# A gated mix of sliding-window attention and a token-mixing MLP: x transposes by DMA into one tensor per block, weights on a second queue, and another order of the work

## The chip, the cores and the metric

The kernel runs on one core of a Trainium2 chip. The core has a matrix engine (TensorE, PE in the views), a vector engine (VectorE, DVE), a scalar engine (ScalarE, ACT), a general-purpose engine (GpSimd, POOL) and SyncE (SP), which here only issues DMAs; sixteen DMA engines move the data. Each engine runs its own instructions strictly in program order and waits at semaphores for the others. PE writes its results to PSUM, which has eight banks; everything else lies in SBUF.

The metric is the device time of one execution in microseconds.

## The reference, cut to what matters

x has 2048 rows (tokens) of 512 elements, bf16. Two results of x are mixed, row by row, with a gate.

```python
def _A_ref(x, wqkv, wo):            # 32 heads of 16, window of 256 keys
    qkv = (x @ wqkv).reshape(B, S, 3, H, Dh).transpose(2, 0, 3, 1, 4)
    q, k, v = qkv[0], qkv[1], qkv[2]
    scores = einsum("bhqd,bhkd->bhqk", q, k) * (Dh ** -0.5)
    mask = (i - j >= 0) & (i - j < 256)
    p = softmax(where(mask, scores, -1e9))
    o = einsum("bhqk,bhkd->bhqd", p, v)
    return o.transpose(0, 2, 1, 3).reshape(B, S, D) @ wo

def _B_ref(x, w1, b1, w2, b2):      # w1: 2048 x 1376, w2: 1376 x 2048
    h = layernorm(x)
    u = gelu(einsum("bsd,sf->bdf", h, w1) + b1)
    y = einsum("bdf,fs->bds", u, w2) + b2
    return y.transpose(0, 2, 1)

g = sigmoid((x * gate_w).sum(-1))
return g * _A_ref(x, ...) + (1 - g) * _B_ref(x, ...)
```

The MLP of B mixes tokens: its first product sums over all 2048 rows of h, so it can't start before the layer norm of every row is done.

## The kernel before, in words

**Tiles and stages.** Rows come in four blocks of 512 (index i) and sixteen groups of 128 (qb for queries, kb for keys). The stages are:

- *Loads.* x by rows into `xo` (`load_x`, line 330), wqkv in four pieces of 128 rows (`load_w`, line 337), w1 in twelve pieces (line 350), wo (line 355), all on SP's queue; a few small vectors on POOL's (line 359 and on). Later w2 (line 731) goes into the same buffer `wb` that held w1, piece by piece, once the chains that read w1 are done.
- *x transposed.* The projections need x with its columns on partitions, the tile `XT`, one tile of four column groups by 2048 rows. Block 0 is transposed by PE from `xo` (line 436) into PSUM and copied to `XT` by ACT or DVE (lines 419 and 420). Blocks 1 to 3 are transposed by DMA from DRAM (line 427), each into its 512 columns of every column group. `BYPE = 1` says how many blocks go by PE.
- *Projections* (`project`). For each block four chains for K, four for Q, four for V; a chain is a sum of four matmuls of 512 columns into one PSUM bank (`chain`, line 462). K is copied to `KT` and V to `VA` (lines 419, 420). Q is multiplied on DVE by two masks of alternating heads into `QZ` (line 502), so that one product with K gives two heads apart.
- *Attention.* For each group of queries qb and each half of the heads hf there are up to three key groups; each triple (qb, hf, kb) is called a piece, 90 in all. A piece is eight S matmuls (line 568) into two pairs of banks, two exps on ACT (line 587), a mask on the diagonal and on the far key group, by DVE (line 598) or POOL (line 602), and sixteen matmuls with V (line 623). The extra column of ones in `VA` gives the softmax's sums; a reciprocal (line 639) and a product (line 646) on DVE normalise into `on`, which has five buffers. A DMA transpose (line 657) puts it, transposed, over the rows of `xo` that are no longer needed.
- *Layer norm.* For each group of 128 rows `bn_stats` and `bn_aggr` on DVE (lines 517, 521), for each block an inverse root on POOL (line 527), then `h` on DVE or POOL (line 534).
- *MLP and end.* Eleven chains u of 16 matmuls (h by w1), each followed by a GELU of five steps on DVE and ACT (lines 312, 703, 708, 715, 720); sixteen chains y of 11 matmuls (w2 by the GELU's result); y is scaled and shifted (lines 310, 313), the chain a (o by wo) is added with the gate (line 754), and the result stored (line 759). The gate is 64 narrow matmuls on `XT` (line 668).

**What sets the order.** Each step is a `Task` with its engine or engines and an expected duration, its dependencies, a priority (lower goes first) and the buffers that it takes. `arrange` simulates the engines and at each step starts the task that can start earliest, within a patience the one of the lowest priority number; where a task may run on two engines it takes the one that finishes it first. The list that comes out is the program order on each engine. `LATENCY` is what it adds to a task's end before a dependent may start: 0.22 us for PE. `ORDER` holds the priorities and `BANKS` the PSUM banks that each kind of chain may take; S takes pairs from all eight. Waits between engines are put in afterwards, from the tiles that instructions read and write.

Of the kernel before, what the change touches and what calls it, by code (L numbers as in the profile page):

```python
# [8 lines left out]
BF16 = mybir.dt.bfloat16  # L9
# [99 lines left out]
def arrange(tasks, patience):  # L109
# [18 lines left out]
    while len(order) < len(tasks):  # L128
# [66 lines left out]
def kernel(  # L195
# [28 lines left out]
    BYPE = 1  # L224
# [8 lines left out]
    XT = sb.tile([P, 4, S], BF16, name="XT")  # L233
# [13 lines left out]
    QZ = sb.tile([P, NQ, 2, 4, SB], BF16, name="QZ")  # L247
# [51 lines left out]
    def add(*a, **k):  # L299
        t = Task(*a, **k)  # L300
        tasks.append(t)
        return t
# [16 lines left out]
    def load(name, emit, kb, q="SP", deps=(), prio=0.0, small=None, issue=0.5):  # L319
        landed[0] += kb / 370.0  # L320
        clock[0] += issue
# [11 lines left out]
    dwk = []  # L333

    def load_w(c):
        dwk.append(load(
            f"wqkv{c}", lambda: nc.sync.dma_start(wqkv[:, c, :], A_wqkv[c * P:(c + 1) * P, :]), 384, prio=0.001 * (c + 1)
        ))

    load_x(0)  # L340
    for c in range(4):
        load_w(c)
    for i in range(1, NSB):
        load_x(i)
# [79 lines left out]
    xt = {}  # L424
    for i in range(BYPE, NSB):
        def emit(i=i):
            nc.sync.dma_start_transpose(XT[:, :, i * SB:(i + 1) * SB], X[i * SB:(i + 1) * SB, :])
        xt[i, 0] = xt[i, 1] = add(f"xt{i}", {"SP": 7.5}, emit, [], 1.05 + 0.1 * i, lat=3.0)
    for i in range(BYPE):
        for c in range(2):  # L430
            b = bank("xt")

            def emit(i=i, c=c, b=b):
                g16 = buf(b).bitcast(BF16)
                return [
                    nc.tensor.transpose(
                        g16[:, (cc * 4 + t) * P:(cc * 4 + t + 1) * P],
                        xo[:, 4 * i + t, (2 * c + cc) * P:(2 * c + cc + 1) * P], ident[:],
                    )
                    for cc in range(2) for t in range(4)  # L440
                ]
# [372 lines left out]
```

## Time and profile before

| | us |
|---|---|
| median of 3 runs | 247.25 (247.23 to 247.72) |
| the profiled execution | 247.16 |
| its span | 245.0 |
| PE busy in it | 216.3 |
| ACT busy | 189.7 |
| DVE busy | 174.2 |
| POOL busy | 61.0 |

How to read the profile: the busy times are those of one profiled execution, on its one core. Its span runs from the first to the last instruction, and the execution's time is a little longer than that. The page cuts the span into 40 slices, 6.1 us each, and gives the busy share of an engine in each as a digit, 9 for 90% or more; PEclk gives PE's clock in the same way, as a share of full speed. In groups of instructions, "out<-in" names the tiles written and read, then come the count, the busy time, the mean duration of one in ns, and the idle time of that engine just before with what ended it. Matmuls overlap in PE's pipeline, so the mean duration of one is longer than its share of the busy time. A few matmul records are missing from the trace, which makes PE's busy time a little too small.

### The profile page before, as it was taken

The page shows a single profiled execution, that of the slowest core. Times are in us where ns is not written, and L with a number is a line of the kernel's source. Part 1 is how long each engine was busy: PE and PEld are TensorE (multiplying, and loading weights), DVE is VectorE, ACT ScalarE, POOL GpSimd, SP SyncE. Part 2 cuts the span into 40 slices and gives each one's busy share as a digit, 9 for nine tenths or more (in the row PEclk, how much of TensorE's full clock was granted, in tenths as well). Part 3 has the DMA queues.
Part 4 walks back from the last instruction along what each step waited for, and adds up shares of the span by engine and source line. Part 5 has one row for each costly group of instructions (what it writes and reads, how often), then busy time and mean ns, then how long its engine had stood idle before and what let it go on. Part 6 is the DMA issues. An engine that isn't in the chain of part 4 may idle for free. (4 is left out here: it accounts for less than half of the span.)

```text
span 245.0 us, 6531 instructions
## 1 busy us (share of the span) xinstructions
PE 216.3 (88%) x2809; PEld 105.1 (43%) x2856; DVE 174.2 (71%) x266; ACT 189.7 (77%) x214; POOL 61.0 (25%) x45
## 2 busy tenths in 40 slices
PE   7006998998999999999999999899999999999993
PEld 3002342634444444444444454345554444444541
DVE  3007899989996788889869688775765776667722
ACT  2004599797999998888999999888788888888821
POOL 8303597089165003333000000603003000030000
PEclk9655999979999999999999999999999999999998
DMA  6994999303011010541018116101003010101111
GB/s 185 225 276 100 287 351 345 100 3 46 1 24 24 0 24 3 165 201 24 0 24 293 54 24 237 24 0 46 24 21 67 24 46 23 47 21 46 45 36 50
DMA packets 26892, 21.66 MB, mean 88 GB/s; under 512 B 15760, under 2 KB 24464, under 8 KB 26864
## 3 DMA queue, kind: packets, MB, share of 16 engines
q1 hardware_dynamic: 26704, 21.24, 29.8%
q8 instruction: 22, 0.36, 0.6%
q0 software_dynamic: 160, 0.01, 0.5%
q14 instruction: 6, 0.05, 0.1%
HBM read 15.47 MB, written 2.10 MB: 72 GB/s over the span
## 5 line engine op out<-in xcount | busy, mean ns | idle before, releaser
L587 ACT ACTIVATE et<-ps 128x1024 bf16<-128x1024 f32 x180 | 170.7, 1039 | 19.1 <-PE ps L568 19.0
L598 DVE TENSOR_TENSOR et<-et,mask 128x2048 bf16<-128x2048 bf16 x47 | 59.0, 1255 | 14.0 <-ACT et L587 13.9
L602 POOL TENSOR_SCALAR_AFFINE_SELECT et<-et 128x2048 bf16<-128x2048 bf16 x13 | 26.1, 2008 | 125.1 <-PE pb L462 43.3
L623 PEld LDWEIGHTS <-et 128*128 128x128 bf16 x1440 | 46.9, 96 | 23.1 <-issue 5.0
L623 PE MATMUL pb<-VA,et 128*128 128x17 bf16 x1440 | 50.1, 171 | 0.8 <-DVE KT L420 0.6
L462 PE MATMUL pb<-XT,wqkv 128*128 128x512 bf16 x120 | 35.2, 402 | 17.0 <-DVE mv L521 15.0
L462 PE MATMUL pb<-h,wb 128*128 128x512 bf16 (+1 forms) x163 | 46.4, 381 | 1.3 <-issue 0.5
L462 PE MATMUL pb<-ug,wb 128*128 128x512 bf16 (+1 forms) x165 | 45.6, 380 | 1.3 <-DVE ot L754 0.4
L462 PEld LDWEIGHTS <-wb 128*128 128x128 bf16 (+2 forms) x352 | 27.8, 98 | 31.8 <-issue 8.7
L568 PE MATMUL ps<-QZ,KT 32*128 32x256 bf16 x720 | 36.1, 275 | 1.6 <-ACT et L587 1.2
L568 PEld LDWEIGHTS <-KT 32*128 32x128 bf16 x720 | 10.7, 92 | 33.4 <-ACT et L587 27.4
L462 PEld LDWEIGHTS <-wqkv 128*128 128x128 bf16 x128 | 11.1, 101 | 32.0 <-DVE mv L521 15.3
L534 POOL TENSOR_SCALAR h<-xo,mv,rstd 128x512 bf16<-128x512 bf16 x9 | 21.7, 2422 | 0.4
L754 DVE SCALAR_TENSOR_TENSOR ot<-pb,gg,bp 128x512 bf16<-128x512 f32 x16 | 12.0, 749 | 13.8 <-PE pb L462 11.7
L502 DVE TENSOR_TENSOR QZ<-pb,par 128x1024 bf16<-128x1024 f32 x16 | 19.2, 1219 | 3.6 <-PE pb L462 3.4
L462 PE MATMUL pb<-wo,xo 128*128 128x512 bf16 x57 | 17.4, 380 | 0.9 <-issue 0.3
L462 PE MATMUL pb<-wqkv,XT 128*128 128x512 bf16 x56 | 16.3, 398 | 0.8 <-issue 0.5
L313 DVE TENSOR_SCALAR bp<-pb,c,c 128x512 f32<-128x512 f32 x13 | 10.5, 808 | 6.1 <-PE pb L462 6.1
L419 ACT ACTIVATE XT<-pb 128x1024 bf16<-128x1024 bf16 x1 | 2.4, 2432 | 16.0 <-DMA XT<-in_A_x_dram 16.0
L646 DVE TENSOR_TENSOR on<-pb,rd 128x256 bf16<-128x256 f32 x32 | 13.6, 424 | 1.1
L517 DVE BATCH_NORM_STATS2 stats<-xo 128x6 f32<-128x512 bf16 x16 | 10.5, 671 | 2.4 <-DMA xo<-in_A_x_dram 2.4
L720 DVE SCALAR_TENSOR_TENSOR ug<-t,uf 128x512 bf16<-128x512 f32 (+1 forms) x11 | 7.5, 685 | 6.1 <-ACT t L715 6.1
(49 smaller groups left out, 106.7 us busy)
## 6 DMA issues: line engine op xcount, KB each, us to landing
wb<-in_B_w_dram SPq DMA_DIRECT2D x8, 512.0 KB, 8.3
wb<-in_B_w_dram SPq DMA_DIRECT2D x2, 2048.0 KB, 7.8
xo<-in_A_x_dram SPq DMA_DIRECT2D x4, 512.0 KB, 11.2
out_dram<-ot SPq DMA_DIRECT2D x16, 128.0 KB, 1.7
wqkv<-in_A_wqkv_dram SPq DMA_DIRECT2D x4, 384.0 KB, 6.4
wb<-in_B_w_dram SPq DMA_DIRECT2D x4, 352.0 KB, 9.3
wb<-in_B_w_dram SPq DMA_DIRECT2D x1, 1024.0 KB, 5.1
wo<-in_A_wo_dram SPq DMA_DIRECT2D x1, 512.0 KB, 4.6
```

The source lines that it names most:

```text
L313: return nc.vector.tensor_scalar(out=out_, in0=in_, scalar1=scale, scalar2=bias, op0=ALU.mult, op1=ALU.add)
L462: nc.tensor.matmul(buf(b)[:rows, :], lhsT=lhsT, rhs=rhs, start=(j == 0), stop=(j == n - 1))
L502: lambda k=k, b=b: nc.vector.tensor_tensor(out=QZ[:, i % NQ, :, k, :], in0=buf(b)[:, None, :].to_broadcast([P, 2, SB]), in1=par[:][:, :, N ...
L517: f"bs{t_}", {"DVE": 0.67}, lambda b=b, t_=t_: nc.vector.bn_stats(buf(b)[:], xo[:, t_, :]),
L534: return eng.tensor_scalar(out=h[:, t_, :], in0=xo[:, t_, :], scalar1=mv[:, t_, 0:1], scalar2=rstd[:, t_:t_ + 1], op0=ALU.subtract, op1=AL ...
L568: made.append(nc.tensor.matmul(buf(b2[r // 2])[:, (r % 2) * 512 + kk * 256:(r % 2) * 512 + kk * 256 + 256], lhsT=KT[32 * r:32 * r + 32, (k ...
L587: lambda j=j, b2=b2, e=e: nc.scalar.activation(out=buf(e)[:, j * 1024:(j + 1) * 1024], in_=buf(b2[j])[:], func=ACT.Exp, scale=SCALE),
L598: return nc.vector.tensor_tensor(out=view, in0=view, in1=mask[:, int(far), None, :].to_broadcast([P, 16, P]), op=ALU.mult)
L602: return nc.gpsimd.affine_select(out=buf(e), in_=buf(e), pattern=[[0, 16], [-1 if far else 1, P]], compare_op=ALU.is_gt if far else ALU.is ...
L623: made.append(nc.tensor.matmul(buf(o)[:, hl * DV:(hl + 1) * DV], lhsT=buf(e)[:, col:col + 128], rhs=VA[:, kb, head, :], start=(first and h ...
L646: lambda rd=rd, o=o, ob=ob, hf=hf: nc.vector.tensor_tensor(out=buf(ob)[:, hf * 256:(hf + 1) * 256].rearrange("p (h d) -> p h d", d=DH), in ...
L754: lambda bp=bp, b=b, ot=ot, qb=qb: nc.vector.scalar_tensor_tensor(out=buf(ot)[:], in0=buf(b)[:], scalar=gg[:, qb:qb + 1], in1=buf(bp)[:], ...
```

## The change

- *`arrange`.* Between two tasks of PE alone the 0.22 us are no longer added: a dependent PE task may follow at once.
- *`ORDER` and `BANKS`.* New priorities; more banks for most kinds of chain.
- *x transposed.* `XT` becomes four tiles, one for each block, and all four blocks are transposed by DMA. PE's transposes of block 0 and their copies go.
- *Loads.* wqkv comes in two pieces, the columns of Q and K together (1 MiB) and those of V (0.5 MiB), issued on ACT's queue. SP issues the transpose of block 0 first, then x 0, x 1, the transpose of block 1, x 2, x 3, four pieces of w1, the transposes of blocks 2 and 3, and the rest as before. The chains of K and Q depend on the first weight piece, those of V on the second.
- *Q layout.* In `QZ` the two masked copies of one Q chain lie side by side.
- *`h`.* Only DVE computes it.
- *The transpose of o* depends on all four h of its block in place of its own.
- One expected duration of y's evacuation on DVE is raised from 0.76 to 0.81.

```diff
@@ arrange
         for n, s in t.next:
             n.left -= 1
-            n.ready = max(n.ready, t.done if s is None else start + s)
+            if s is not None:
+                n.ready = max(n.ready, start + s)
+            elif list(n.engines) == ["PE"] == [e]:
+                n.ready = max(n.ready, end)
+            else:
+                n.ready = max(n.ready, t.done)
 ORDER = dict(
-    k=52.18, q=78.76, v=68.4, u=1.2, u_step=18.14, y=84.32, a=47.23, pv=6.7, s=5.8, to=100.63, gate=229.14,
-    lead=0.63, block=67.65, xt=-11.08, patience=0.17, m=60.31, ln=98.99, ev=60.19, gelu=2.68, w1=4.9,
+    k=-36.13, q=-39.5, v=-35.98, u=131.85, u_step=8.5, y=122.66, a=-17.68, pv=-21.07, s=-48.88, to=90.92,
+    gate=3.01, lead=-8.24, block=86.1, patience=0.13, m=46.84, ln=275.69, ev=8.39, gelu=97.56, w1=0.04,
 )
 BANKS = dict(
-    qkv=(5, 6, 7),
-    u=(6, 7),
-    y=(4, 5),
-    a=(4, 5),
-    pv=(6, 7),
-    to=(6, 7),
-    xt=(0, 1, 2, 3, 4, 5, 6, 7),
+    qkv=(4, 5, 6, 7),
+    u=(4, 5, 6, 7),
+    y=(7, 6, 5, 4, 3),
+    a=(2, 3, 4, 5, 6, 7),
+    pv=(0, 1, 2, 3, 4, 5, 6, 7),
+    xt=(4, 5),
 )
...
-    XT = sb.tile([P, 4, S], BF16, name="XT")
+    XT = [sb.tile([P, 4, SB], BF16, name=f"XT{i}") for i in range(NSB)]
...
-    QZ = sb.tile([P, NQ, 2, 4, SB], BF16, name="QZ")
+    QZ = sb.tile([P, NQ, 4, 2, SB], BF16, name="QZ")
...
-    dwk = []
-
-    def load_w(c):
-        dwk.append(load(
-            f"wqkv{c}", lambda: nc.sync.dma_start(wqkv[:, c, :], A_wqkv[c * P:(c + 1) * P, :]), 384, prio=0.001 * (c + 1)
+    def load_w(name, a, z, prio):
+        return load(
+            name, lambda: nc.scalar.dma_start(wqkv[:, :, a:z], A_wqkv[:, a:z].rearrange("(c p) n -> p c n", p=P)),
+            z - a, prio=prio, q="ACT",
+        )
+
+    xt = []
+
+    def load_t(i, prio):
+        landed[0] += 512 / 250.0
+        xt.append(add(
+            f"xt{i}", {"SP": 1.9}, lambda: nc.sync.dma_start_transpose(XT[i][:], X[i * SB:(i + 1) * SB, :]), [], prio,
+            lat=max(2.2, landed[0] - clock[0] - 1.9),
         ))
-
+        clock[0] += 1.9
+
+    load_t(0, 0.0)
+    dwk = load_w("wqk", 0, 2 * D, 0.0)
+    dwv = load_w("wv", 2 * D, 3 * D, 0.01)
     load_x(0)
-    for c in range(4):
-        load_w(c)
-    for i in range(1, NSB):
-        load_x(i)
+    load_x(1)
+    load_t(1, 0.015)
+    load_x(2)
+    load_x(3)
+    load_t(2, ORDER["w1"] + 0.045)
+    load_t(3, ORDER["w1"] + 0.095)
...
-    xt = {}
-    for i in range(BYPE, NSB):
-        def emit(i=i):
-            nc.sync.dma_start_transpose(XT[:, :, i * SB:(i + 1) * SB], X[i * SB:(i + 1) * SB, :])
-        xt[i, 0] = xt[i, 1] = add(f"xt{i}", {"SP": 7.5}, emit, [], 1.05 + 0.1 * i, lat=3.0)
-    for i in range(BYPE):
-        for c in range(2):
...
-            t = add(f"xt{i}{c}", {"PE": 0.55}, emit, [dx[i], k1], ORDER["xt"] + i, takes=[b])
-            xt[i, c] = copy_out(
...
@@ project
-                b, t = chain(f"v{t_}", mms, dwk + [xt[i, 0], xt[i, 1], warm, k5], prio, "qkv")
+                b, t = chain(f"v{t_}", mms, [dwv, xt[i], warm, k5], prio, "qkv")
...
-            b, t = chain(f"{kind}{k}_{i}", mms, dwk + [xt[i, 0], xt[i, 1], warm] + old, prio, "qkv")
+            b, t = chain(f"{kind}{k}_{i}", mms, [dwk, xt[i], warm] + old, prio, "qkv")
...
-                        out=QZ[:, i % NQ, :, k, :], in0=buf(b)[:, None, :].to_broadcast([P, 2, SB]),
+                        out=QZ[:, i % NQ, k, :, :], in0=buf(b)[:, None, :].to_broadcast([P, 2, SB]),
...
-                eng = nc.vector if engine[0] == "DVE" else nc.gpsimd
-                return eng.tensor_scalar(
+                return nc.vector.tensor_scalar(
...
-            hready.append(add(f"h{t_}", {"DVE": 0.41, "POOL": 0.75}, emit_h, [pw], ORDER["ln"] - 0.5 + i))
+            hready.append(add(f"h{t_}", {"DVE": 0.41}, emit_h, [pw], ORDER["ln"] - 0.5 + i))
...
-                            rhs=QZ[32 * r:32 * r + 32, (qb // 4) % NQ, :, k, (qb % 4) * P:(qb % 4 + 1) * P],
+                            rhs=QZ[32 * r:32 * r + 32, (qb // 4) % NQ, k, :, (qb % 4) * P:(qb % 4 + 1) * P],
...
-                rel[qb] + [hready[qb]], ORDER["to"], lat=2.5, uses=[ob],
+                rel[qb] + hready[4 * (qb // 4):4 * (qb // 4) + 4], ORDER["to"], lat=2.5, uses=[ob],
...
-            f"yb{qb}", {"ACT": 0.72, "DVE": 0.76},
+            f"yb{qb}", {"ACT": 0.72, "DVE": 0.81},
```

More of the change, by code (lines that the diff above doesn't have):

```diff
@@ L223 @@
     NK = 3
-    BYPE = 1
     X = A_x[0]
@@ L320, in load @@
         landed[0] += kb / 370.0
-        clock[0] += issue
+        clock[0] += issue if q == "SP" else 0.0
         lat = small if small is not None else landed[0]
@@ L480, in project @@
                 t_ = 4 * i + k
[L481 to L482 removed]
+                mms = [(XT[i][:, ck, k * P:(k + 1) * P], wqkv[:, ck, 2 * D:3 * D], P) for ck in range(4)]
+                b, t = chain(f"v{t_}", mms, [dwv, xt[i], warm, k5], prio, "qkv")
                 vready[t_] = copy_out(
@@ L673, in emit_gate @@
         ]
-    gt = add("gate", {"PE": 1.8}, emit_gate, [k3] + list(xt.values()), ORDER["gate"], takes=[gb])
+    gt = add("gate", {"PE": 1.8}, emit_gate, [k3] + xt, ORDER["gate"], takes=[gb])
     ga = add("gateact", {"ACT": 0.25}, lambda: nc.scalar.activation(th[:], buf(gb)[:, 0:NT], ACT.Tanh, scale=0.5), [gt], 4, uses=[gb])
```

21 lines of the change are left out of this document (2 added, 19 removed).

## The prediction

> **What bounds the kernel now.** I read the page first, for the share of each engine and its course over the span.
>
> ```profile
> span 245.0 us, 6531 instructions
> PE   7006998998999999999999999899999999999993
> PEclk9655999979999999999999999999999999999998
> ```
>
> TensorE (PE) is at 9 tenths or more in nearly every slice from the fourth on, and idle in slices 2 and 3. So the second view is the list of PE's waits, and the third the timeline of the first 30 us.
>
> ```profile
> PE pb L462 <- DVE mv L521: 15.0, 1, 15.0
> PE pb L462 <- issue: 1.9, 12, 0.2
> ...
> PE pb L462 <- DVE QZ L502: 0.6, 1, 0.6
> ...
> PE pb L462 <- DVE KT L420: 0.3, 1, 0.3
> ```
>
> ```profile
> 0.79 0.40 SPq L330 DMA_DIRECT2D xo<-in_A_x_dram  x1
> 1.25 3.60 PE L411 MATMUL pb<-zeros 128*128 128x512 bf16 x8 [1.25 <-DVE eps L366]
> 1.26 1.83 SPq L337 DMA_DIRECT2D wqkv<-in_A_wqkv_dram  x4
> ...
> 3.13 2.03 SPq L330 DMA_DIRECT2D xo<-in_A_x_dram  x3
> ...
> 4.63 1.14 PE L436 MATMUL pb<-ident,xo 128*128 128x128 bf16 x16
> ...
> 5.21 19.42 SPq L427 DMA_TRANSPOSE XT<-in_A_x_dram  x3
> ...
> 18.24 2.43 ACT L419 ACTIVATE XT<-pb 128x1024 bf16<-128x1024 bf16 x1 [15.96 <-DMA XT<-in_A_x_dram]
> 18.25 2.42 DVE L420 COPY XT<-pb 128x1024 bf16<-128x1024 bf16 x1 [12.77 <-DMA XT<-in_A_x_dram]
> ...
> 20.73 5.85 PE L462 MATMUL pb<-XT,wqkv 128*128 128x512 bf16 x16 [14.96 <-DVE mv L521]
> ...
> 28.88 1.95 ACT L587 ACTIVATE et<-ps 128x1024 bf16<-128x1024 f32 x2
> ```
>
> PE finishes its 16 transposes at 5.77 us. Their two copies out of PSUM start only at 18.24, released by a DMA that writes XT: the transpose of block 1, queued behind 3.5 MiB of loads. The copies write columns 0 to 511 and that DMA columns 512 to 1023 of the same tile, so the copies waited for data they don't touch. The first projection starts when they end, at 20.73 (the view names mv, the last small DVE instruction before it). That wait is 15.0 of PE's 22; the other eight entries are 1.9 us down to 0.3. The end is PE's too, by the chain of work that ended last:
>
> ```profile
> 236.94 4.36 PE pb L462 x19
> ...
> 241.38 0.75 DVE ot L754
> ```
>
> So PE works from 20.73 to 241.30, 220.6 us, almost without a gap; then come 3.7 us (the last combination, its store, the end of the span). The profiled execution took 247.16, 2.2 more than its span; the median of three is 247.25, so a forecast for the one holds for the other.
>
> **The change, part by part.** Where DVE is tight and what the phases cost stands in these rows, stretches first (columns: width, busy time of PE, PEld, DVE, ACT, POOL, granted clock, DMA share, GB/s), then groups:
>
> ```profile
> 1.00:7.40 6.40, 4.52 (x24) 2.15 (x24) 1.93 (x8) 1.27 (x2) 6.26 (x10) 1.00 0.80 248
> 7.40:9.50 2.10, 0.00 (x0) 0.00 (x0) 0.00 (x0) 0.00 (x0) 0.79 (x1) 0.69 1.01 232
> 9.50:12.70 3.20, 0.00 (x0) 0.00 (x0) 0.00 (x0) 0.00 (x0) 0.00 (x0) 0.50 1.05 168
> ...
> 20.73:25.30 4.57, 4.57 (x11) 1.63 (x12) 2.73 (x6) 0.60 (x1) 3.03 (x3) 0.50 0.79 179
> 20.73:73.10 52.37, 48.59 (x634) 22.89 (x646) 47.91 (x88) 42.36 (x50) 31.94 (x20) 0.92 0.52 147
> 45.80:52.60 6.80, 6.64 (x125) 3.24 (x122) 5.99 (x14) 6.45 (x9) 2.55 (x3) 0.75 0.01 4
> ```
>
> ```profile
> L587 ACT ACTIVATE et<-ps 128x1024 bf16<-128x1024 f32 x180 | 170.7, 1039 | 19.1 <-PE ps L568 19.0
> L598 DVE TENSOR_TENSOR et<-et,mask 128x2048 bf16<-128x2048 bf16 x47 | 59.0, 1255 | 14.0 <-ACT et L587 13.9
> ...
> L623 PE MATMUL pb<-VA,et 128*128 128x17 bf16 x1440 | 50.1, 171 | 0.8 <-DVE KT L420 0.6
> ...
> L568 PE MATMUL ps<-QZ,KT 32*128 32x256 bf16 x720 | 36.1, 275 | 1.6 <-ACT et L587 1.2
> ...
> L534 POOL TENSOR_SCALAR h<-xo,mv,rstd 128x512 bf16<-128x512 bf16 x9 | 21.7, 2422 | 0.4
> L502 DVE TENSOR_TENSOR QZ<-pb,par 128x1024 bf16<-128x1024 f32 x16 | 19.2, 1219 | 3.6 <-PE pb L462 3.4
> ...
> L646 DVE TENSOR_TENSOR on<-pb,rd 128x256 bf16<-128x256 f32 x32 | 13.6, 424 | 1.1
> L517 DVE BATCH_NORM_STATS2 stats<-xo 128x6 f32<-128x512 bf16 x16 | 10.5, 671 | 2.4 <-DMA xo<-in_A_x_dram 2.4
> ...
> L639 DVE RECIPROCAL rd<-pb 128x16 f32<-128x16 f32 x32 | 8.0, 250 | 4.1 <-PE pb L623 4.0
> ...
> L420 DVE CAST KT<-pb 128x512 bf16<-128x512 f32 x8 | 5.3, 676 | 0.2 <-PE pb L462 0.2
> ...
> L534 DVE TENSOR_SCALAR h<-xo,mv,rstd 128x512 bf16<-128x512 bf16 x7 | 3.4, 514 | 0.0
> L521 DVE BATCH_NORM_AGGREGATE mv<-stats 128x2 f32<-128x6 f32 x16 | 2.7, 174 | 0.0
> ```
>
> *The front.* 16 PE transposes (1.14 us) and two copies (2.4 us side by side) go. Block 0 now needs its transpose DMA, first on SP's empty queue, and the Q and K weights (1 MiB), first on ACT's. Both are issued from about 0.8 us. The stretches give what the DMA engines deliver then: 6.40 x 248 = 1.59 MB by 7.40, and 2.10 x 232 = 0.49 MB more by 9.50. If only these 1.5 MiB (1.57 MB) move, they are in at 7.4; if block 0 of x, next on SP's queue, has moved too (2.10 MB), at 9.5. So PE starts between 7.4 and 9.5; I take **9.0**, nearer the late end, because these are the rates of plain loads, and between the last byte and the waiting engine some time passes that they don't show.
>
> [...] No row of before shows two such queues at work.
>
> A DMA transpose on SP can hold it long: the three above hold it for 19.42 us, the first behind the loads. In the new order SP issues transpose 0, x 0, x 1, transpose 1, x 2, x 3, four pieces of w1, transposes 2 and 3, the rest. What transpose 1 holds up is x 2 and x 3, wanted by the layer norm only; transposes 2 and 3 pass behind 2 MiB of w1, wanted by projections that come after two blocks of attention. I cost both at nothing; the cover is those projections' lateness, and if block 1's were late, PE would idle after some 10 us of block 0. The weight issues, 1.83 us on SP, go to ACT, idle there.
>
> *The clock.* The projections ran at a granted clock of 0.50 until 25.30, 11 matmuls in 4.57 us where full speed would take half: 2.3 lost. In the new kernel the warm-up ends at 4.85, and after 9.0 the clock has to rise again: the same loss, so 0 (bounds -2.3 if it never falls, 0).
>
> *DVE.* h moves to DVE alone: nine more at 0.514, +4.6 us, and POOL sheds 21.7. DVE is 47.91 of 52.37 busy before the first matmul of the MLP at 73.1, so this isn't covered everywhere. Layer norm costs 16 x (0.671 + 0.174 + 0.514) = 21.7 us on DVE and now ranks last there (ln = 275.69, the masks 46.84). The MLP needs all of h, so what counts is how long PE lives on other work. Projections of three blocks: 36 chains of four matmuls at 0.22 (the chain above, 4.36 us for 19, has 0.23 with the last one's drain in it) = 31.7, plus 2.3 for the clock and 1.8 for the gate (its row stands below): 35.8. One attention piece costs PE 8 x 36.1/720 + 16 x 50.1/1440 = 0.96, and ACT two exps of 170.7/180 = 1.90. Exps start 8.15 us after the projections, as before (28.88 - 20.73): at 17. If h is complete at T, PE idles (T - 9) - 35.8 - 0.96 (T - 17)/1.9 = 0.495 T - 36.2, nothing up to **T = 73**. From about 9.5 to 17 DVE has little else, so half the layer norm fits there. For the other 10.9 us it has what attention leaves: per block of 24 pieces 16 masks (20.1), eight pairs of reciprocal and division (5.4), four QZ (4.9) and half of eight evacuations at about 0.7 (2.8), 33.2 us in 45.6, a gap of 0.27: 40 us, T = 57. With no half of the evacuations taken by ACT it is 0.21 and T = 69. So nothing is lost by this sum; before's own T, 73.1, gives 0 too. That one lies right at the point, so I take **+0.6** (T = 74), bounds 0 and 4 (T = 81).
>
> *The order.* The views of the tiles XT and xo say when the gate's matmuls and the products with wo run:
>
> ```profile
> L668 PE MATMUL pb<-gwc,XT x64: 163/163/177, 46.8 to 48.4; 128*128 128x1 bf16 x64
> L462 PE MATMUL pb<-wo,xo x57: 376/379/390, 165.9 to 240.9; 128*128 128x512 bf16 x57
> ```
>
> A chain's pieces are planned without a latency between them, PSUM banks are shared more widely, and priorities are new. PE's instructions stay the same, so its 220.6 us change only by waits; the seven listed after 20.73, from 1.9 down to 0.3, sum to 5.7, a bound on the gain, and I take 0. The gate's 64 short matmuls are followed by a dip of the clock (0.75 in the mean from 45.80 to 52.60, that is half speed for 3.4 us, 1.7 lost): bounds -1.7 and 0.
>
> *The rest.* The QZ layout moves the same 1024 elements per instruction (1.219 us) and the S matmuls read the same columns: 0, at most the 0.6 us that PE waited for QZ once. The transposes of o now wait for four rows of h, not one; behind them on SP stand other such transposes, w2 and the stores. The product with wo first runs at 165.9, far behind h, so these wait for nothing new. What could hurt is the five buffers of o: were h of block 0 late, they would stay taken and attention would stop behind them. h of block 0 is the first to be ready, so 0. The mask and evacuation prices in the planner change nothing by themselves.
>
> Sum: 9.0 + 220.6 + 3.7 + 2.2 + 0.6 = **236.1 us**, 11.1 less. Its own range, from 7.4 with the dip gone to 9.5 with T = 81, is 232.2 to 240.0.
>
> **The rivals.**
>
> *A wait for wv (239.2).* The wait that goes was one between disjoint columns of one tile.
>
> ```profile
> ACT XT L419 <- DMA XT<-in_A_x_dram: 16.0, 1, 16.0
> ```
>
> wqkv stays one tile, and its two loads interleave: columns 0 to 1023 and 1024 to 1535 of each of four row groups. If the same rule holds, the K and Q chains wait for wv as well. Then 2.5 MiB have to move: 3.20 x 168 = 0.54 MB more, at 12.7; PE starts there, and 12.7 + 226.5 = 239.2. For it speaks that row; against it, that reads may be tracked more finely than writes, and that wv may land early anyway.
>
> *h too late (over 240, slower than before from a point).* One mechanism: layer norm, last on DVE, gets none of its work done before attention starts. Then 21.7 us have to fit into gaps of 0.21 to 0.27 from 17 on: T = 97 to 120. PE would idle 0.495 T - 36.2: 12 to 23 us, 247 to 259. It turns slower than before at T = 73 + 11.7/0.495 = 97. For it: DVE's 47.91 of 52.37 and ln = 275.69. Against: x 0 and x 1 stand early in SP's queue, the planner starts what is ready, and POOL, freed of 21.7 us, can take masks. Halfway cases lie between 240 and 247.
>
> *The clock stays (231.6).* PE starts at 7.4, before the clock falls, and the 2.3 us are saved too: 235.5 - 1.6 - 2.3. The clock was still full at 7.4 and 0.69 in the mean to 9.50, so it would be close.
>
> *It doesn't do it (247).* The first transpose is held or moves slowly beside the weights, and PE starts near 20 again. The first stretches' 248 GB/s speak against.
>
> **How the numbers follow.** Forecast 0.52; wait for wv 0.18; h too late 0.20, of it 0.12 still faster than before and 0.08 slower; the clock stays 0.08; no effect 0.02. Range 231.6 to 242.5: out are half of the clock case, the h cases above 242.5 and no effect, under 0.2. A measurement of this kernel can tell 0.2% from no change; faster by that 0.90, within it 0.02, slower 0.08.
>
> **What would show it.** The first projection on PE between 7.4 and 9.5, with XT0 or wqkv named as releaser; near 12.7 with wv as the last landing means the first rival. A granted clock of 0.5 over the first projections confirms the ramp. The first MLP matmul (h, wb) before 73 with PE at 9 tenths throughout confirms the middle; a gap ahead of it, released by h, the second rival. PE's work from its first projection to its last matmul should again take 220 to 222 us. If it takes much less, I mis-sized waits that hid in PE's busy time; if more, new ones came with the order.

## The result, and the profile after

The changed kernel takes 237.94 us, the median of four runs (237.26 to 238.1); the kernel before took 247.24 beside it. The ratio is 0.962, with a 95% interval of 0.959 to 0.964. The forecast was 236.1. Here and below a time is the median of a kernel's runs; two of the six runs of the longer warm-up, 237.73 and 671.09 us, lie more than 1.5% above its fastest and are left out of its time. The profiled execution took 238.0 us with a span of 235.6, so 2.4 lie outside the span.

The page of the changed kernel: the span, and the busy share of PE and its clock in 40 slices.

```profile
span 235.6 us, 6549 instructions
...
PE   6299998999976999989999999999999999999993
...
PEclk9999997999996599999999999999999999999999
```

The hole in slices 2 and 3 has shrunk to most of slice 2. A new hole stands in slices 12 and 13, with a lower clock in 13 and 14, from about 68 to 82 us in all. The list of PE's waits names both:

```profile
PE pb L452 <- DMA XT<-in_A_x_dram: 5.6, 1, 5.6
PE ps L556 <- ACT et L575: 3.8, 7, 1.2
...
PE ps L556 <- DVE on L634: 1.0, 1, 1.0
PE pb L611 <- ACT et L575: 0.8, 2, 0.5
```

In place of the 15.0 us for XT's copies there are 5.6 us for the transpose of block 0. New are seven waits of S pieces for exps. The timeline of the front (start, duration, engine, line, operation; idle time before it and its releaser):

```profile
0.81 1.40 SPq L347 DMA_TRANSPOSE XT<-in_A_x_dram  x1
...
6.54 0.11 PEld L452 LDWEIGHTS <-wqkv 128*128 128x128 bf16 x1 [2.59 <-DMA wqkv<-in_A_wqkv_dram]
...
6.69 8.36 SPq L347 DMA_TRANSPOSE XT<-in_A_x_dram  x1
...
10.43 5.30 PE L452 MATMUL pb<-XT,wqkv 128*128 128x512 bf16 x16 [5.58 <-DMA XT<-in_A_x_dram]
...
17.39 0.40 PE L556 MATMUL ps<-QZ,KT 32*128 32x256 bf16 x8
```

The Q and K weights are there at 6.54, the transposed block only at 10.4, though it was issued at the same time and is half as large. The first projection starts at 10.43 in place of 20.73. PE's last matmul ends at 231.78 and the last combination starts there, so PE's stretch is 221.35 us long against 220.6 before. The sum of the profiled runs: 10.3 us gained in the front, 0.8 lost in PE's stretch, 0.1 in the tail (3.8 for 3.7), 0.2 outside the span (2.4 for 2.2): 9.2.

The new hole in the stretches (width; PE, PEld, DVE, ACT, POOL; granted clock; DMA share, GB/s), and then PE's timeline inside it:

```profile
68.30:77.40 9.10, 5.38 (x138) 3.25 (x138) 8.37 (x19) 9.10 (x11) 2.77 (x3) 0.70 0.01 2
71.98:82.22 10.24, 7.97 (x90) 3.00 (x90) 7.30 (x14) 8.74 (x10) 1.21 (x2) 0.50 0.08 16
82.30:231.80 149.50, 148.84 (x1999) 74.21 (x1998) 109.40 (x152) 130.98 (x148) 12.25 (x6) 1.00 0.20 62
```

```profile
68.76 0.40 PE L556 MATMUL ps<-QZ,KT 32*128 32x256 bf16 x8 [0.40 <-ACT et L575]
...
70.59 1.38 PE L611 MATMUL pb<-VA,et 128*128 128x17 bf16 x48 [0.52 <-ACT et L575]
72.42 0.61 PE L556 MATMUL ps<-QZ,KT 32*128 32x256 bf16 x8 [0.46 <-ACT et L575]
...
77.39 1.01 PE L452 MATMUL pb<-h,wb 128*128 128x512 bf16 x2
```

From 68.3 to 77.4 ACT is busy without a break, and PE has nothing but attention: the five S pieces there wait 0.30 to 1.22 us each until an exp has read their banks. PE is idle 9.10 - 5.38 = 3.7 us there, and its clock falls to half for 10.24 us, in which it is busy 7.97 us that would take about half at full speed. From 82.3 on PE is hardly ever idle: it is busy 148.84 of 149.50. The first MLP matmul ends the hole at 77.4; the group of h says why it didn't come sooner:

```profile
L522 DVE TENSOR_SCALAR h<-xo,mv,rstd x16: 400/404/2117, 33.5 to 75.9; 128x512 bf16<-128x512 bf16 x16
```

The last h starts at 75.9 and takes 0.4 us (before, the MLP began at 73.1).

### The profile page after: what moved, and what is told of

The parts are those of the page before. It is cut to its first block, busy times and chain, and to the rows that moved or that the text cites. A ratio compares the mean times of both kernels' runs of the same rounds, so it can differ in the third digit from the quotient of the medians.

```text
span 235.6 us, 6549 instructions
## 1 busy us (share of the span) xinstructions
PE 219.1 (93%) x2840; PEld 106.2 (45%) x2840; DVE 170.2 (72%) x266; ACT 190.7 (81%) x218; POOL 44.1 (19%) x39
## 4 chain that ended last, share of the span: by engine, by line
PE 79%; ACT 8%; DVE 5%; DMA 4%; issue 1%; ACTq 0%; DVEq 0%
PE pb L452 55%; PE pb L611 13%; PE ps L556 11%; ACT et L575 8%; DMA XT<-in_A_x_dram 4%; DVE h L522 1%; DVE t L696 1%; DVE b1c L418 1%; DVE stats L506 0%; DVE QZ L491 0%; DVE on L634 0%; DVE uf L315 0%; DVE ot L742 0%; DVE t L691 0%; DVE KT L437 0%
## 5 line engine op out<-in xcount | busy, mean ns | idle before, releaser
L590 POOL TENSOR_SCALAR_AFFINE_SELECT et<-et 128x2048 bf16<-128x2048 bf16 x16 | 32.3, 2020 | 155.9 <-ACT et L575 155.9
L586 DVE TENSOR_TENSOR et<-et,mask 128x2048 bf16<-128x2048 bf16 x44 | 53.6, 1219 | 10.3 <-ACT et L575 10.1
L452 PEld LDWEIGHTS <-wb 128*128 128x128 bf16 (+2 forms) x352 | 30.8, 99 | 37.9 <-issue 9.4
L611 PEld LDWEIGHTS <-et 128*128 128x128 bf16 x1440 | 41.3, 96 | 12.0 <-issue 4.3
L611 PE MATMUL pb<-VA,et 128*128 128x17 bf16 x1440 | 43.6, 171 | 0.8 <-ACT et L575 0.8
L452 PE MATMUL pb<-XT,wqkv 128*128 128x512 bf16 x128 | 32.9, 396 | 5.7 <-DMA XT<-in_A_x_dram 5.6
L627 DVE RECIPROCAL rd<-pb 128x16 f32<-128x16 f32 x32 | 8.1, 252 | 16.0 <-PE pb L611 15.8
L436 ACT ACTIVATE KT<-pb 128x512 bf16<-128x512 f32 x8 | 4.8, 602 | 12.7 <-PE pb L452 12.7
L316 DVE TENSOR_SCALAR bp<-pb,c,c 128x512 f32<-128x512 f32 x10 | 8.1, 808 | 4.2 <-PE pb L452 4.1
L506 DVE BATCH_NORM_STATS2 stats<-xo 128x6 f32<-128x512 bf16 x16 | 10.3, 676 | 0.0
L313 ACT ACTIVATE bp<-pb,c,c 128x512 f32<-128x512 f32 x6 | 4.7, 776 | 6.9 <-issue 4.4
```

The costliest lines, as they stand in the source:

```text
L316: return nc.vector.tensor_scalar(out=out_, in0=in_, scalar1=scale, scalar2=bias, op0=ALU.mult, op1=ALU.add)
L452: nc.tensor.matmul(buf(b)[:rows, :], lhsT=lhsT, rhs=rhs, start=(j == 0), stop=(j == n - 1))
L506: f"bs{t_}", {"DVE": 0.67}, lambda b=b, t_=t_: nc.vector.bn_stats(buf(b)[:], xo[:, t_, :]),
L586: return nc.vector.tensor_tensor(out=view, in0=view, in1=mask[:, int(far), None, :].to_broadcast([P, 16, P]), op=ALU.mult)
L590: return nc.gpsimd.affine_select(out=buf(e), in_=buf(e), pattern=[[0, 16], [-1 if far else 1, P]], compare_op=ALU.is_gt if far else ALU.is ...
L611: made.append(nc.tensor.matmul(buf(o)[:, hl * DV:(hl + 1) * DV], lhsT=buf(e)[:, col:col + 128], rhs=VA[:, kb, head, :], start=(first and h ...
```

## The experiments

Three theories stood at the start. *T1*: the gain is the false wait between columns of one tile, and nothing else. *T2*: the new hole comes from an overloaded DVE, so that less work there, or the layer norm earlier, recovers it. *T3*: the hole lies in the order, and the exps pace it. The front was a question of its own: what holds the first block until 10.4.

**The tile split alone.** The kernel before, with `XT` as four tiles; loads, order, PE's transposes of block 0 and everything else stay.

```diff
-    XT = sb.tile([P, 4, S], BF16, name="XT")
+    XT = [sb.tile([P, 4, SB], BF16, name=f"XT{i}") for i in range(NSB)]
```

> The kernel before with XT as four tiles and nothing else: block 0 still transposed by TensorE, all loads still on SP's queue, the order on every engine unchanged. Theory 1, the wait for columns that nobody touches made the hole at the start: the copies of block 0 start when TensorE has transposed (5.8 us in place of 18.2), the first projection waits only for the last of the four weight pieces and starts at 10 to 12 us, and the time falls to 236.5 to 239. Rival, the second queue or the DMA transpose is needed: the first projection stays later than 15 us and the time stays above 243.

It took 236.7 us (ratio 0.9615, 0.9557 to 0.9673): the whole gain of the change. PE's timeline, and the stretches of this kernel and then of the changed one:

```profile
8.32 2.31 PE L462 MATMUL pb<-XT,wqkv 128*128 128x512 bf16 x5 [2.53 <-DVE mv L521]
11.64 4.22 PE L462 MATMUL pb<-XT,wqkv 128*128 128x512 bf16 x11 [1.01 <-DMA wqkv<-in_A_wqkv_dram]
...
17.95 0.40 PE L568 MATMUL ps<-QZ,KT 32*128 32x256 bf16 x8
```

```profile
50.00:90.00 40.00, 39.45 (x542) 18.93 (x543) 33.64 (x51) 37.00 (x43) 12.76 (x8) 1.00 0.09 18
90.00:230.00 140.00, 138.27 (x1821) 66.90 (x1819) 99.45 (x139) 117.87 (x133) 14.81 (x8) 1.00 0.21 65
```

```profile
50.00:90.00 40.00, 35.83 (x523) 17.07 (x524) 32.00 (x59) 36.84 (x41) 8.39 (x7) 0.87 0.09 18
90.00:230.00 140.00, 139.37 (x1869) 69.54 (x1868) 103.84 (x145) 122.97 (x140) 12.25 (x6) 1.00 0.21 66
```

T1 holds for the time: all other edits together sum to nothing that this comparison can tell from zero. They are not nothing one by one. (What they do without the split was not run.) From 50 to 90 us the old order keeps PE busy 39.45 of 40 us at full clock, the new one 35.83 at 0.87. Behind 90 the new order issues more in the same 140 us: 1869 matmul records for 1821.

**The layer norm earlier.**

```diff
-    ln=275.69
+    ln=20.0
```

> The changed kernel with the priority of the layer norm at 20 in place of 275.69, so that on VectorE it goes ahead of the masks. Theory 2, TensorE ran short between 68 and 77 us because the last h came at 76: the first MLP matmul comes before 68 us, the waits of TensorE on exps in that stretch and the half clock after it go, and the time falls by 3 to 6 us, to 232 to 235. Rival, VectorE simply has too much work there and what is taken from the masks holds up attention instead: the time stays within 1 us of 238.

A miss: 242.19 us (0.982, 0.978 to 0.986). The stretches, and the wait:

```profile
68.30:77.40 9.10, 8.30 (x111) 3.65 (x110) 5.49 (x10) 9.10 (x11) 0.00 (x0) 1.00 0.04 8
...
220.00:240.00 20.00, 9.98 (x145) 4.53 (x143) 6.49 (x11) 8.96 (x10) 2.01 (x1) 0.65 0.11 27
```

```profile
PE pb L452 <- DMA xo<-on: 3.3, 1, 3.3
```

The first MLP matmul came at 69.3 and the hole went, as expected. It came back at the end: there the last attention pieces run with nothing beside them, and PE waits 3.3 us for the last transposed o.

**Statistics over 64 of 512 columns.** This takes work from DVE and leaves the order alone; the layer norm is computed from an eighth of each row.

```diff
-nc.vector.bn_stats(buf(b)[:], xo[:, t_, :])
+nc.vector.bn_stats(buf(b)[:], xo[:, t_, 0:64])
```

> The changed kernel with the layer norm's statistics taken over 64 of the 512 columns (so its means and variances are of those columns only); the order on every engine is unchanged. Theory 2 in its narrow form, the hole of TensorE before 77 us is VectorE arriving late with h: with some 8 us less work on VectorE the last h comes 4 to 8 us earlier, the seven waits of TensorE on exps between 68 and 77 us shrink from 3.7 us to under 1, the half clock after them goes, and the time falls by 4 to 6 us, to 232 to 234. Rival, which the run with the earlier layer norm leaves possible: the work only moves, and TensorE runs short at the end in its place, so the time stays above 236.

A miss again: 237.4 us (0.9618, 0.9579 to 0.9658). The group of the statistics (least, median and greatest ns, first and last start), and the wait:

```profile
L506 DVE BATCH_NORM_STATS2 stats<-xo x16: 186/217/228, 16.0 to 69.6; 128x6 f32<-128x64 bf16 x16
```

```profile
PE ps L556 <- ACT et L575: 3.8, 7, 1.2
```

A statistic takes 217 ns in place of 676, yet the last one still starts at 69.6 (71.2 in the changed kernel) and the last h at 74.7 (75.9), and the seven waits are the same 3.8 us. T2 falls as far as it blames the amount of DVE's work. DVE runs its list in order (in the changed kernel's trace all its 266 instructions start in the order of the program), and the last statistics stand behind masks, reciprocals and divisions: over this run DVE waits 10.1 us for exps before masks, and 18.5 us before reciprocals for the matmuls with V, which need the exps.

**h on DVE or POOL**, with POOL at 0.75 us in the planner.

```diff
-add(f"h{t_}", {"DVE": 0.41}, emit_h, ...)
+add(f"h{t_}", {"DVE": 0.41, "POOL": 0.75}, emit_h, ...)
```

> The changed kernel with h on VectorE or GpSimd again, as in the kernel before; nothing else. Theory 2: VectorE is relieved by some of 16 x 0.55 us before 76 us, the last h comes 1 to 4 us earlier and the time falls by 0.5 to 3 us. Rival: the h on GpSimd takes 2.1 to 2.4 us each, comes as late or later, and the time is 238 or more.

It took 238.99 us (0.969, 0.964 to 0.974). Twelve h went to POOL at a median of 2.09 us, the last starting at 80.6, and the MLP began at 80.5. That is 1 us above the changed kernel, with intervals that touch: POOL doesn't help here, and makes the last h later.

**Chunk 0 of the MLP pulled into the hole.** Its first piece waits for h 0 to 11 only and goes ahead of the S pieces.

```diff
             d = list(deps) if last is None else [last]
+            d += [x for y in late[a:a + piece] for x in y]
...
-emit, d, prio - 0.001 * a,
+emit, d, -60 if name == "u0" and a == 0 else prio - 0.001 * a,
...
-        b, t = chain(f"u{fc}", mms, dw1[g] + hready, ORDER["u"] + ORDER["u_step"] * fc, "u")
+        b, t = chain(f"u{fc}", mms, dw1[g], ORDER["u"] + ORDER["u_step"] * fc if fc else 131.85, "u", late=[hready[:12]] + [[x] for x in hready[1:]])
```

> The changed kernel with one difference in the plan: a piece of the first layer's accumulation waits only for the h tiles that it reads (its first piece for tiles 0 to 11), and the first piece of chunk 0 goes ahead of the S pieces; the other pieces of chunk 0 keep their low priority. The order of the rest follows from the planner. Theory 1, the hole at 68 to 77 us is lost time of its own (3.7 us of waits for the exps and some 2 of half clock), because TensorE has no other work there: with the first MLP matmuls inside the hole they start near 70 instead of 77.4, the waits for exps in that stretch fall under 2 us, and the time is 233 to 236. Theory 2, the MLP's matmuls are the only work that can lie under the exps, and there are just enough of them: what is spent in the hole is missing later, so a hole of the same kind comes back behind 190 us, as in the run with the layer normalisation earlier, and the time is 238 to 243. I hold theory 2 the likelier.

It took 245.89 us (0.996, 0.993 to 0.998), worse than either theory had it. The MLP began at 73.6, not near 70. The last stretch, and the wait in it:

```profile
225.00:244.00 19.00, 10.12 (x150) 5.12 (x150) 6.75 (x10) 8.77 (x10) 0.00 (x0) 0.81 0.13 36
```

```profile
PE pb L452 <- DMA xo<-on: 3.8, 1, 3.8
```

As with the earlier layer norm, idle time comes back where the last attention pieces run alone. PE is idle about 5 us between 225 and the end of its last matmul at 240.2; in the changed kernel it is busy without a break from 225 to the end. The direction is that of theory 2. The other 3 us of the 8 lost aren't explained: the planner reorders everything behind such an edit. Two edits that filled the hole in the new order, wholly or in part, both lost more at the end, so *T3* stands: the hole lies in the order. Whether an order without either loss exists for this structure stays open.

**The Q layout of before.**

```diff
-    QZ = sb.tile([P, NQ, 4, 2, SB], BF16, name="QZ")
+    QZ = sb.tile([P, NQ, 2, 4, SB], BF16, name="QZ")
```

> The changed kernel with the old layout of QZ; the order on every engine is unchanged. I expect no difference, 237.5 to 238.5. Rival, writes of one Q chain collide with reads of another in the old layout, as they did in XT: TensorE waits on QZ and the time is 239 or more.

237.86 us (0.963, 0.959 to 0.967): no difference.

**The V weights on SP's queue**, behind x 0; ACT's queue carries only Q and K. The order of the work is unchanged.

```diff
+            if i == 0:
+                nc.sync.dma_start(wqkv[:, :, 2 * D:], A_wqkv[:, 2 * D:].rearrange("(c p) n -> p c n", p=P))
```

> The changed kernel with the V weights issued on SP's queue behind x 0 in place of ACT's second; order on the engines otherwise unchanged. Theory 3, the DMA engines take packets of the two queues in turn, so the transpose's packets of 256 bytes lose against the weights' of 1 and 2 KB: with 0.5 MiB less beside it transpose 0 lands 1.0 to 1.7 us earlier, the first projection starts at 8.7 to 9.4 us and the time falls by about as much, to 236.3 to 237. Rival A, the transpose takes its 9.6 us whatever runs beside it: start 10.4, time 238. Rival B, the K and Q chains wait for the V weights too, since the two loads interleave in one tile: the second weight load or matmul of the first chain waits until these land, 11.5 us or later, and the time is 239 or more.

It took 235.71 us (0.9551, 0.9516 to 0.9585), a little better than expected, and better than both kernels. PE's timeline:

```profile
8.47 6.50 PE L454 MATMUL pb<-XT,wqkv 128*128 128x512 bf16 x16 [3.92 <-DMA XT<-in_A_x_dram]
14.88 1.89 PE L454 MATMUL pb<-wqkv,XT 128*128 128x512 bf16 x8
16.70 0.40 PE L558 MATMUL ps<-QZ,KT 32*128 32x256 bf16 x8
```

With 0.5 MiB less beside it the block lands 2 us sooner. The V weights landed at 14.84, while the K and Q chains ran without a stall, so these don't wait for other columns of the same weight tile. But a start 1.96 us earlier gave a first S only 0.69 earlier: the 16 projections take 6.50 us in place of 5.30, and the V chains, which start at 14.88, couldn't have started before their weights were there.

**The weights of the split-only kernel on ACT's queue.** One edit against the first experiment.

```diff
-lambda: nc.sync.dma_start(wqkv[:, c, :], A_wqkv[c * P:(c + 1) * P, :])
+lambda: nc.scalar.dma_start(wqkv[:, c, :], A_wqkv[c * P:(c + 1) * P, :])
```

> The kernel before with XT as four tiles, as in the first run, and the four weight pieces issued on ACT's queue; the order on the engines is unchanged. Theory 3, the two queues take turns on the same DMA engines: x 1 to 3 and transpose 1 now move beside the weights, which land later, so the first unbroken run of projections starts at 12.5 to 14.5 us in place of 11.6, and the time is 1 to 3 us longer than the first run's 236.7. Rival, the second queue brings the weights in sooner: it starts before 10.5 us and the time is 235 to 236.

It took 240.79 us (0.975, 0.972 to 0.978), 4.1 more than with one queue, where 1 to 3 were expected. The waits:

```profile
PE pb L462 <- DMA wqkv<-in_A_wqkv_dram: 4.6, 2, 2.5
```

On one queue the weights came ahead of x 1 to x 3. On a queue of their own they share the engines with them, and their last packet is through at 15.25 us in place of 10.21. The granted clock then stays at half until 21.89 in place of 15.06, and the first S comes at 23.04 in place of 17.95.

**The old order in the new structure**: the V weights on SP, with `ORDER`, `BANKS` and the 0.22 us of before.

```diff
-    k=-36.13, q=-39.5, v=-35.98, u=131.85, ...
+    k=52.18, q=78.76, v=68.4, u=1.2, ...
```

> The changed kernel with the V weights on SP behind x 0, and with the priorities, the banks and the latency of the kernel before. Theory 4, the new order is worth nothing in sum, since what it gains after 90 us it loses before h is ready: without it the first MLP matmul comes near 60 us, TensorE's stalls between 50 and 90 us fall from 6.5 to 1 or 2 us and those after 90 us rise from 1 to 4, and the time is 234 to 236.5, within 1.2 us of 235.7. Rival, the new order carries part of the gain: 238 or more.

A bad miss: 263.25 us (1.066, 1.064 to 1.068). The waits:

```profile
PE ps L554 <- ACT et L573: 6.2, 9, 1.4
PE pb L609 <- DVE on L632: 5.3, 3, 2.1
```

The MLP began at 87.9. The same priorities gave 236.7 us in the structure that they belong to. So the order can't be judged apart from it: an expected duration or an engine more, and the same numbers give another program.

**Only the K weights beside block 0.** The Q and V columns follow the block on SP's queue, ahead of x 0.

```diff
+        if i == 0:
+            for a in (0, 2 * D):
+                nc.sync.dma_start(wqkv[:, :, a:a + D], A_wqkv[:, a:a + D].rearrange("(c p) n -> p c n", p=P))
```

> The kernel with the V weights on SP's queue (235.71 us, first projection at 8.47) with the loads cut once more: only the K columns of the projection weights (0.5 MiB) stay on ACT's queue beside the first transposed block; the Q columns and then the V columns follow the block on SP's queue, ahead of the rows of x for the statistics. The order of the matmuls is the same. Theory 1, the first projection waits for the bytes that are in flight beside it and for nothing else: with 1 MiB in place of 1.5 the first projection starts at 6.5 to 7.5, the Q columns are there before the second chain needs them, and the time is 234 to 235.2. Theory 2, the transposed block is bound by its own packets: the start stays within 0.4 us of 8.47, the second chain waits for the Q columns, and the time is 235.5 to 237. I hold theory 1 the likelier.

The start went as theory 1 has it, the time didn't: 236.56 us (0.9585, 0.9561 to 0.9609). PE's timeline, and the stretch of the half clock:

```profile
7.32 1.74 PE L458 MATMUL pb<-XT,wqkv 128*128 128x512 bf16 x4 [2.79 <-DMA XT<-in_A_x_dram]
10.03 4.86 PE L458 MATMUL pb<-XT,wqkv 128*128 128x512 bf16 x12 [0.97 <-DMA wqkv<-in_A_wqkv_dram]
...
16.55 0.40 PE L562 MATMUL ps<-QZ,KT 32*128 32x256 bf16 x8
```

```profile
7.49:14.32 6.83, 5.86 (x15) 1.85 (x14) 1.23 (x1) 1.19 (x2) 0.25 (x1) 0.50 1.05 236
```

A start 1.15 us earlier brought the first S 0.15 forward: the second chain waited 0.97 for the Q columns, and the clock rose only at 14.32. In the kernel with the V weights on SP, with the other start, it rose at the same place. The granted clock of that kernel, by stretches of PE (width; PE; granted clock; DMA share, GB/s):

```profile
7.51:14.34 6.83, 5.87 (x14) 0.50 0.96 204
38.23:41.64 3.41, 3.41 (x16) 0.50 1.14 347
72.37:79.20 6.83, 4.99 (x77) 0.50 0.00 0
```

Each stretch of half clock is a multiple of 3.41 us: 3.41, 6.83, and 10.24 in the changed kernel's hole. That gave a last theory: the clock is decided at the end of each 3.41 us, and rises only behind a stretch that PE has filled. Both starts, 7.32 and 8.47, left a gap of 1.0 us in the stretch up to 10.9, and paid for the next one.

**A longer warm-up**, 20 matmuls for 8, on the kernel with the V weights on SP, and then **the V weights ahead of x 0** as well.

```diff
-for _ in range(8)],
+for _ in range(20)],
```

> The kernel with the V weights on SP's queue (235.71 us) with 20 warm-up matmuls in place of 8; the order of everything else is the same. The question is the half clock over the first projections. Theory 1, the clock is decided at the end of stretches of 3.41 us, and becomes full only behind a stretch that TensorE filled: the records of all runs are multiples of 3.41 us (3.42, 6.83, 10.24, 17.06), and the run with the K weights first started 1.1 us earlier and still became fast at the same 14.3 us. Then the longer warm-up, which fills the stretch up to some 8 us, lets the first 16 projections run at full speed: they take 3.6 in place of 6.5 us, and the record shows full speed from 7 to 8 us on. The V weights land only at about 14.9, so the V chains wait for them, and of the 2.9 us only 0 to 1 is left in the time: 234.7 to 235.8. Theory 2, the half speed of the first projections has another cause (the transfers beside them, or a ramp that starts with the projections): they take 6.5 us again, and the time is 235.5 to 236.5.

> The same with the V weights ahead of the first rows of x on SP's queue, so that they follow the transposed block at once. If theory 1 of the run before holds, the V weights land at 11 to 12.5, the V chains start at about 12 and the first S comes at 13.5 to 14.5 in place of 16.7; the rest is the same order shifted forward, and the time is 232.5 to 234. The hole near 70 us comes 2 to 3 us earlier and stays. If theory 2 holds, the time is that of the run before within 0.5 us. A risk in both: the statistics get their rows 1.5 us later, which the order has room for at the start (DVE is busy 6.4 of the first 20 us).

The first took 234.07 us (0.948, 0.945 to 0.952), 0.6 under the range of theory 1. PE's timeline:

```profile
1.26 6.58 PE L430 MATMUL pb<-zeros 128*128 128x512 bf16 x20 [1.26 <-DVE eps L385]
8.06 3.61 PE L454 MATMUL pb<-XT,wqkv 128*128 128x512 bf16 x16 [0.23 <-DMA XT<-in_A_x_dram]
12.29 1.89 PE L454 MATMUL pb<-wqkv,XT 128*128 128x512 bf16 x8 [0.62 <-DMA wqkv<-in_A_wqkv_dram]
14.11 0.40 PE L558 MATMUL ps<-QZ,KT 32*128 32x256 bf16 x8
```

The second took 233.43 us (0.946, 0.943 to 0.949), the lowest of all, though the intervals of the two overlap:

```profile
7.85 3.61 PE L454 MATMUL pb<-XT,wqkv 128*128 128x512 bf16 x16 [0.78 <-DMA XT<-in_A_x_dram]
...
13.13 0.40 PE L558 MATMUL ps<-QZ,KT 32*128 32x256 bf16 x8
```

In both, the 16 projections take 3.61 us in place of 6.50: twelve more matmuls of zeros, which lie under a wait for DMA, are worth 2.9 us there, and theory 1 holds. What they are worth in the time is less clear. The first S comes 2.59 us earlier in the first run (14.11 for 16.70), but the V weights, loaded as before, landed at 12.25 in that profiled execution and not at 14.84; had they come at 14.84 again, the V chains would have waited for them. In the second run, whose V weights land at 9.9, nothing waits for these, and the first S comes at 13.13. A stretch needn't be filled to the last for the clock to rise: in the second run it is full from 3.99, though PE's first matmul came only at 1.26, 0.7 us after such a stretch would have begun. The hole stays: its seven waits are 4.0 us in the second run.

## Why the prediction came out as it did

The forecast is 1.8 us under the result, and faster as forecast. Nearly all of the difference is the front, 1.4 us; the tail and the time outside the span are 0.3. PE's stretch of 221.35 us is within 0.2 of the forecast's 220.6 + 0.6, but that is luck: two of its terms missed effects of several us, which cancelled.

- *What bounds the kernel.* Right: the 15.0 us wait was a false one between columns of a tile, and removing it alone gives the gain.
- *The front*, taken as 9.0 from bounds of 7.4 to 9.5. **It failed by 1.4 us**: the start was 10.43, beyond the late end. Part of the 1.4 is chance: five other kernels with the same loads beside block 0 started at 9.60 to 10.70 in their profiled executions, all beyond the late end. The step let all bytes come in from 1.0 us on, at the rate of plain loads. In the trace's packet records the first packet of the weights moves at 1.94 us, the first of the transpose only at 4.64, and its last is through at 9.19, 1.2 us before PE starts. Between 7 and 8 us the queues moved (packets, MB, share of the 16 engines' time; q10 is ACT's queue, q1 SP's):

```profile
q10 hardware_dynamic: 281, 0.29, 80.9%
q1 hardware_dynamic: 284, 0.07, 31.9%
```

  That is about as many packets of each, of 256 bytes for the transpose and of 1 KB for the weights, so the transpose got a fifth of the bytes. From 5 to 7 us, 701 of its packets moved beside 339, some 28% of the bytes; how the DMA engines choose between the queues is not shown. With 1 MiB of weights beside it in place of 1.5 the start was 8.47 (8.06 and 8.60 in two other kernels), with 0.5 it was 7.32. A second queue can also cost: the split-only kernel lost 4.1 us by it (240.79 for 236.7), since it lost the order that one queue gave, and its weights were through at 15.25 in place of 10.21.
- *The clock*, taken as the same ramp with 0 gained. Off by little here: eight matmuls ran at half speed before 13.95, 11 in before. But the reason was wrong: it isn't a fixed ramp. In these runs the loss went with how the start lay to the stretches of 3.41 us, 14 half-speed matmuls with the start at 8.47 or eight with that at 10.43, and a warm-up that nearly reached the first projection (to 7.84, for a start at 8.06) removed it (3.61 us for 6.50); the rival *the clock stays* had priced that at 2.3.
- *DVE*, taken as T = 74 and +0.6. **It failed in size.** The mechanism is the one that the step priced: PE has nothing but attention until h is complete. h was complete at 76.3, for which the formula 0.495 T - 36.2 gives 1.6. The row shows 3.7 us of idle time, and the half clock behind it, up to 4 us more (half of the 7.97 busy ones), wasn't in the step. The formula also spreads PE's work evenly up to T. In the order that ran, 160 of the 192 matmuls of the projections are done by 68.4 (the other 32 come at 141.8), and what is left is attention at the pace of ACT. The split-only kernel, which has no such hole, had done 126 of them by 70, and its MLP began at 62.8. Nor was it the amount of DVE's work: 7.3 us less of it (16 x 0.459) changed nothing, while another place for the layer norm in DVE's list had h complete at 69.3 and no hole there, though the kernel was slower for its end. The rival *h too late* named this hole, but its price was for a DVE that starts the layer norm late, and the runs speak against that: the first statistics ran at 17.0.
- *The order*, taken as 0, with the seven listed waits of 5.7 us as a bound on the gain. **That bound was mis-sized**, since the list has only what shows as idle time. In the traces a matmul of 512 columns is drawn at least 376 ns long, while at full speed the next starts 215.5 ns after it, so short gaps don't show. An estimate from the starts of all matmuls, with the lower quartile of the distance for each pair of shapes as full speed, gives 207 us for the split-only kernel, whose matmuls are those of before; so some 14 of before's 220.6 were gaps and half clock. About 4 of these are the half clock after 20.73 and behind the gate, 5.7 the listed waits, and the rest is in no list. In the changed kernel the losses by this estimate are 2.2 up to 30 us, 2.1 to 50, 6.6 to 90, and 2.3 behind 90; in the split-only kernel 5.6, 3.1, 1.6 and 5.4. That is the trade: 3.1 us gained behind 90 and 4.4 before 50 (2.1 of it given back by the later start, 10.43 for 8.32), against 5.0 lost from 50 to 90. My 0 was near the sum of terms that I didn't see.
- *The gate's dip* stayed, as taken (half clock from 37.8 to 41.2, behind the gate at 35.65). PE's stretch of 221.35 us lies in the 220 to 222 named as the test, and that test proved weak: it can't tell two effects that cancel from no effect.
- *The rest*: the Q layout is worth 0, as taken, and the transposes of o hold nothing up.
- *The rival of a wait for wv* is false: K and Q chains ran while the V columns were still in flight.

## What to carry to other kernels

A tile that several DMAs write in column slices should be several tiles: that single edit was worth 10 us here, as much as the whole change that it belongs to. Two full queues moved about as many packets each and not as many bytes in two of the traces (281 and 284 above, though 701 and 339 before that; in the split-only kernel with two queues 503 of 3 KB and 499 of 4 KB from 2 to 15 us), so what is needed first belongs alone or first on one queue, above all when its packets are small (with 1.5, 1 and 0.5 MiB beside block 0 the start was 10.43, 8.47 and 7.32); and a warm-up of PE should last until its first real matmul (with 20 matmuls for 8 the first 16 projections took 3.61 us for 6.50). A view's waits of an engine that is "busy" are not all its waits: compare the distances of the starts with full speed before an order is costed at nothing. And an order belongs to its program: the old priorities in the new structure took 263.25 us.

## What the runs showed of the hardware

- The half clock came in stretches of 3.41 us: 3.41 behind the gate, 6.83 at the start of six of the kernels, 10.24 in the changed kernel's hole, 13.65 and 17.06 at the start of the split-only kernel with two queues and of before (this row: the kernel before, 8.20 to 25.26).

```profile
8.20:25.26 17.06, 4.53 (x11) 0.50 0.80 190
```

  The recorded full-speed stretches are multiples too: 23.89, 30.72 and 153.6 us in the changed kernel's trace (7, 9 and 45 times 3.413), 3.41, 23.89 and 191.15 in that of before (1, 7 and 56 times). The stretches don't begin at a fixed time: with the same warm-up from 1.26 us on the recorded clock rises anywhere from 3.99 to 5.52. That a part of any small difference can so be luck is my estimate: the same hole cost two stretches with the old Q layout and three in the changed kernel, at times that agree (237.86 and 237.94).
- The gate's 64 matmuls of one column, 1.7 us, are followed by a stretch of half clock in 12 of the 14 profiled kernels. In the other two a boundary of the stretches, counted on from the rise of the clock at the start, falls inside the gate (at 35.01 in the kernel with the earlier layer norm, at 42.37 in the split-only one with two queues). In a third it does so too, with the dip, so why stays open.
- The record of the granted clock can miss the start. In the changed kernel's trace it begins at 13.88, and the view shows full speed while PE runs nine matmuls in 3.52 us, 0.39 each, where full speed has 0.2155:

```profile
10.43:13.95 3.52, 3.52 (x9) 1.27 (x9) 0.00 (x0) 0.60 (x1) 0.00 (x0) 1.00 1.00 232
```

- The transposes of x by DMA started late and held the queue that issues them. In the ten kernels that issue block 0's transpose first, at 0.8 us, its first packet moves at 4.29 to 4.72; the loads on the other queue, issued at the same time, move from 1.9 on. In the changed kernel the first transpose took 1.40 us to issue on SP, the second 8.36 behind two blocks of x; nothing that SP had to issue after it was urgent here.
